# One turn for the sinks of four heads, in a tile shared with the weights' conversion, and new ordering numbers for the first chunks

## Chip, core and metric

The kernel runs on one core of a Trainium2 chip. The core has five engines with queues of their own: TensorE (PE; its loads of the stationary operand are listed as PEld), VectorE (DVE), ScalarE (ACT), GpSimd (POOL) and SyncE (SP), which here only issues DMAs. The metric is the device time of one execution in microseconds, the median of several runs.

## What is computed

Attention with a few sink positions and a sliding window, and behind it a two-layer network whose gate is `h * cos(h)`:

```python
# q, k, v: (4, 8, 768, 64), n_sink = 4, window = 128
scores = q @ k.T / sqrt(D)
keep = (pos_k < n_sink) | ((0 <= pos_q - pos_k) & (pos_q - pos_k < window))
a = softmax(where(keep, scores, -1e9))          # with 1e-9 added to the sum
x = (a @ v).transpose(0, 2, 1, 3).reshape(3072, 512)
h = x @ w_in                                    # w_in (512, 2048)
out = (h * cos(h)) @ w_out                      # w_out (2048, 512)
```

q, k and v are float32. The weights arrive as 64-bit floats, which the kernel turns into pairs of float32 tiles on the chip.

## The kernel before

The 3072 rows are cut into twelve chunks of 256 (`NT`). The chunks that begin a batch of the first three batches come first; the rest follow batch by batch. For a chunk the kernel does attention for eight heads and then the network in eight slots of 256 hidden columns (`NSLOT`).

Products that must be exact to float32 are made of three products of rounded parts (`hi` and `lo`). A slot is 24 hidden products (`h`, line 390), a chain over ACT and DVE (`yt`, `r`, the sine, the gate, `ghi`, `glo`, lines 399 to 429) and 12 output products (`acc`, line 438). `glo` is the last reader of a slot's PSUM bank, so a later slot's hidden products wait for it; the slots of the first two chunks take turns on two banks, the later ones on three.

The weights come in 32 pieces. SP loads a piece into one of two tiles `raw`; DVE builds float32 in one of two tiles `wt` (lines 491, 497, 503), ACT rounds the upper part (line 524), and DVE or POOL subtracts (line 527). Later each piece is loaded once more and checked for very small entries (line 542), which writes its products into a `wt` tile as scratch.

Attention of a head: masked scores (line 856), exponentials (line 865), normalization (line 883 or 885), which is done for groups of four heads in most chunks; PE turns the probabilities (`tp`, line 945), and PE multiplies by v (`av`). The first 24 heads (the three early chunks) go a shorter way: the probabilities stay whole (`pt`), x is split into `xhi` and `xlo`, and PE subtracts the rounded half in PSUM (line 326) before `xlo` is read.

Chunks that are not the first of a batch have sink columns: the eight columns P to SW of the probabilities are taken apart from the window. Before the change a pair of heads shares one turn. `sink_cols` (lines 915, 917) writes the rounded columns of the pair and their remainders to `gc`, a tile of its own of 48 columns per row block; `sink_turn` (line 927) turns the two row blocks on PE into `gp`; `sink_out` copies `gp` to `gt` on ACT or DVE (line 379 or 381); `values` (line 999) then multiplies `gt` by the head's part of `vs`, which `vs_parts` (lines 905, 906) makes once per batch from the first eight rows of v. Rows of `gt` that belong to the other head of the pair meet zeros in `vs`.

Every step is handed to a planner (`Plan.add`) with its possible engines, an assumed duration and a due time; `Plan.order` walks through time and, on each engine, takes the ready step that is due first. The order it finds is written out as it is: the engines' queues are in order on the chip. Due times are sums of numbers in the table `C`; steps that may go to POOL or DVE (such as line 527) are weighed by `POOLPEN`, `POOLF` and others. 160 filler products (`idle`, line 1262) keep PE occupied at the start; they are due last, so the planner puts them wherever PE would have nothing else.

Of the kernel before, what the change touches and what calls it, by code (L numbers as in the profile page):

```python
# [16 lines left out]
P = 128  # L17
NSINK = 8
SW = P + NSINK
GR = 32 + 2 * NSINK  # L20
# [11 lines left out]
    "SAME": -0.209, "SE": -1.813, "SEM": 0.31, "SPE": 0.11, "STEP": 6.272, "T": 6.142, "TE": [-1.145, 6.142, 6.142],  # L32
    "TQ": 6.142, "VE": 5.203, "WARM": 4, "WI": -19.801, "WO": 7.156, "WS": 2.329, "WS2": 0.23, "WT": 2, "XE": 4.169,
    "XV": 2,
# [134 lines left out]
def attn_moe_kernel(ctx, tc, q, k, v, n_sink, window, w_in, w_out, out):  # L169
# [52 lines left out]
    lims = cp.tile([1, 2, 2, 2], F32, name="lims")  # L222
    tiny = cp.tile([P, NC * NSLOT // 2 + NFT], F32, name="tiny")
# [310 lines left out]
    def check_piece(plan, prio, k, src):  # L534

        add, buf = plan.add, plan.buf
        r, bt = buf("raw", C["RAW"]), buf("wt", C["WT"])
        raw, t32 = raws[r.nth], f32(wts[bt.nth])
# [9 lines left out]
        j = add((("DVE", dve(WP) + 0.02),), least, [i, bt], prio, port=True)  # L548
        r.users += [i, j]
        bt.users.append(j)  # L550
        return j
# [59 lines left out]
    def banded_path():  # L611
# [9 lines left out]
        gc = env.gc = ap.tile([P, CB, GR], F32, name="gc")  # L621
        vs = env.vs = ap.tile([P, NP, 2, 2, D], F32R, name="vs")
# [54 lines left out]
        def load_batch_v(o):  # L677
            def fn(e):
                o.vs32 = xb.rearrange("p (n d) -> p n d", d=D)
                for h in range(2):  # L680
                    for dup in range(2):
                        r0 = h * 32 + dup * 8
                        nc.sync.dma_start(
                            out=o.vs32[r0 : r0 + 8], in_=v[o.b, h::2, 0:NSINK, :].rearrange("p s d -> s p d")
                        )
            return fn
# [214 lines left out]
        def vs_parts(o):  # L901
            def fn(e):
                for h in range(2):
                    r = slice(h * 32, h * 32 + 2 * NSINK)
                    nc.vector.tensor_copy(out=vs[r, :, h, 0, :], in_=o.vs32[r])
                    nc.vector.tensor_tensor(
                        out=vs[r, :, h, 1, :], in0=o.vs32[r], in1=f32(vs)[r, :, h, 0, :], op=ALU.subtract
                    )
            return fn

        def sink_cols(o, o1):
            def fn(e):
                j0 = o.sj[0]
                for h, oo in enumerate((o, o1)):
                    nc.vector.tensor_copy(out=gc.bitcast(F32R)[:, j0:, h * 32 : h * 32 + NSINK], in_=oo.p[:, j0:, P:SW])
                for h, oo in enumerate((o, o1)):
                    nc.vector.tensor_tensor(
                        out=gc[:, j0:, h * 32 + NSINK : h * 32 + 2 * NSINK], in0=oo.p[:, j0:, P:SW],
                        in1=gc[:, j0:, h * 32 : h * 32 + NSINK], op=ALU.subtract,
                    )  # L920
            return fn

        def sink_turn(o):
            def fn(e):
                o.gp = ps.tile([GR, NT], F32, name=f"gp_{o.tag}", tag="av")
                for n, j in enumerate(o.sj):
                    nc.tensor.transpose(  # L927
                        out=o.gp[:, n * P : (n + 1) * P], in_=gc[:, j], identity=ident,
                    )
            return fn  # L930

        def sink_out(o, o1):
# [47 lines left out]
        def values(o):  # L980


            def fn(e):
# [10 lines left out]
                if o.sj:  # L994
                    lhs = vs[:, o.pair, o.odd].rearrange("p a d -> p (a d)")
# [39 lines left out]
        w_in_ready, w_out_ready = {}, {}  # L1035
# [4 lines left out]
        def before_softmax(g, o):  # L1040
# [3 lines left out]
            if o.i0 == CB and o.h == 0:  # L1044
# [7 lines left out]
                o.vt = add([("DVE", 1.1)], vs_parts(o), [i, o.bvs], t - T + 3.4, port=True)  # L1052
# [113 lines left out]
        def after_softmax(g, o):  # L1166
# [34 lines left out]
            if o.sj and o.odd == 0:  # L1201
                o1 = heads[g + 1]
                bg, o.bgt, bgp = buf("g", 1), buf("gt", 1), buf("av", 1)
                e1 = add([("DVE", 0.5)], sink_cols(o, o1), o.nm + o1.nm + [bg], t + DA + 0.5, port=True)
                o.bp.users.append(e1)
                o1.bp.users.append(e1)
                e2 = add([("PE", 0.107 * len(o.sj))], sink_turn(o), [e1, bgp], t + DA + 1.0)
                bg.users.append(e2)
                e3 = add([("ACT", act(NT, False)), ("DVE", dve(NT))], sink_out(o, o1), [e2, o.bgt], t + DA + 1.2)
# [10 lines left out]
            if o.sj:  # L1220
                oe = o if o.odd == 0 else heads[g - 1]
# [56 lines left out]
        for m, (t, (ready, ss), piece) in enumerate(sorted(pieces, key=lambda w: w[0])):  # L1278
            i = weight_piece(plan, t, *piece, guard=False, first=m < C["PL"])
            for s in ss:  # L1280
# [185 lines left out]
```

## Time and profile before

| | us |
|---|---|
| runs | 762.22 (median), 759.51 and 763.29 |
| profiled execution | 762.47 |
| its span, first to last instruction | 760.5 |
| PE busy | 737.3 |
| DVE busy | 622.7 |
| ACT busy | 573.9 |
| POOL busy | 104.4 |

The span is about 2 us shorter than the execution's own time, which includes what lies around the program. Busy times are sums over the span: they do not say in which stretch an engine was full, for which the busy time by stretch is read. A row of the timeline has the start, the duration, the engine, the line, the operation and the tiles, and in brackets the idle time before it with what ended it. Durations of PE overlap: a product that lasts 0.28 us can be followed by the next one 0.12 us later, so the distance of two starts says what one costs.

### The profile page before, as it was taken

To read this page: it belongs to the slowest core of one execution; us is meant where nothing else is said; L and a number is where in the kernel's file an instruction comes from. 1 tells how busy PE (TensorE), PEld (TensorE's weight loads), DVE (VectorE), ACT (ScalarE), POOL (GpSimd) and SP (SyncE) were. 2 spreads that over 40 slices of the span, in tenths; PEclk is the share of its full clock that TensorE was granted. 3 is DMA by queue.
4 is the path that set the end of the run, shared out by engine and by line. 5 is a ranking of instruction groups with operands and counts; after the bars stand their busy time and mean duration, and the time that the engine had idled before them with its cause. 6 is when DMAs were issued, how large, how long until landed. Compare 5 with 4: busy or idle time off the path is not lost.

```text
span 760.5 us, 15290 instructions
## 1 busy us (share of the span) xinstructions
PE 737.3 (97%) x5013; PEld 667.1 (88%) x5013; DVE 622.7 (82%) x1645; ACT 573.9 (75%) x1361; POOL 104.4 (14%) x174
## 2 busy tenths in 40 slices
PE   9979998999999999999999999999999999999996
PEld 8767877889989999998999899989999999999995
DVE  6899999678889899999899998987888988864331
ACT  3887986867978878878788788788688788784322
POOL 2101100001121121121221111111021112110000
PEclk9999999999999999999999999999999999999999
DMA  5664563331455446447356443232242233110000
GB/s 155 186 188 153 162 190 117 77 60 32 101 133 130 90 112 173 115 111 195 81 130 168 101 102 55 46 70 35 51 84 48 50 77 55 22 44 2 24 5 33
DMA packets 215673, 71.51 MB, mean 94 GB/s; under 512 B 204320, under 2 KB 204320, under 8 KB 215584
## 3 DMA queue, kind: packets, MB, share of 16 engines
q1 hardware_dynamic: 215296, 70.43, 38.1%
q8 instruction: 42, 0.69, 0.4%
q14 instruction: 47, 0.39, 0.2%
q10 hardware_dynamic: 288, 0.00, 0.0%
HBM read 64.10 MB, written 6.29 MB: 93 GB/s over the span
## 4 chain that ended last, share of the span: by engine, by line
PE 78%; DVE 10%; ACT 5%; DMA 3%; issue 2%; SPq 0%; POOL 0%; DVEq 0%; POOLq 0%; ACTq 0%
PE h L390 30%; PE acc L438 29%; PE av L999 5%; PE s L843 4%; PE tp L945 4%; DVE wt L503 2%; ACT p L865 2%; DVE wt L497 2%; PE idle L1262 1%; DVE p L856 1%; PE gp L927 1%; PE s L787 1%; DMA raw<-in_moe_w_out_dram 1%; DMA raw<-in_moe_w_in_dram 1%; PE av L975 1%
## 5 line engine op out<-in xcount | busy, mean ns | idle before, releaser
L390 PE MATMUL h<-xhi,whi_in 128*128 128x256 f32 x768 | 224.3, 292 | 3.5 <-DVE glo L429 3.5
L390 PE MATMUL h<-xlo,whi_in 128*128 128x256 f32 x768 | 217.3, 283 | 0.0
L390 PE MATMUL h<-xhi,wlo_in 128*128 128x256 f32 x768 | 217.1, 283 | 0.0
L438 PE MATMUL acc<-whi_out,ghi 128*128 128x512 f32 x384 | 159.0, 414 | 0.0
L390 PEld LDWEIGHTS h<-xhi,whi_in 128*128 128x128 f32 x768 | 146.4, 191 | 9.3 <-DVE glo L429 5.1
L438 PE MATMUL acc<-wlo_out,ghi 128*128 128x512 f32 x384 | 151.0, 393 | 0.0
L438 PE MATMUL acc<-whi_out,glo 128*128 128x512 f32 x384 | 150.5, 392 | 0.0
L390 PEld LDWEIGHTS h<-xhi,wlo_in 128*128 128x128 f32 x768 | 146.7, 191 | 3.8 <-issue 0.5
L390 PEld LDWEIGHTS h<-xlo,whi_in 128*128 128x128 f32 x768 | 146.5, 191 | 0.0
L399 ACT ACTIVATE yt<-h 128x512 int32<-128x512 f32 x96 | 57.2, 596 | 67.9 <-PE h L390 67.0
L405 DVE SCALAR_TENSOR_TENSOR r<-h,yt 128x512 f32<-128x512 f32 x96 | 65.8, 685 | 44.1 <-ACT yt L399 44.0
L865 ACT ACTIVATE p<-p,st 128x264 f32<-128x264 f32 (+1 forms) x192 | 93.5, 488 | 0.5
L856 DVE CUSTOM_DVE_ANT_0 p<-s,mk 128x264 f32<-128x264 f32 (+1 forms) x192 | 75.5, 400 | 20.5 <-PE s L843 14.0
L438 PEld LDWEIGHTS acc<-whi_out,glo 128*128 128x128 f32 x384 | 72.1, 188 | 16.2
L438 PEld LDWEIGHTS acc<-whi_out,ghi 128*128 128x128 f32 x384 | 72.6, 189 | 7.7 <-issue 0.7
L438 PEld LDWEIGHTS acc<-wlo_out,ghi 128*128 128x128 f32 x384 | 72.9, 190 | 7.2 <-issue 0.7
L412 ACT ACTIVATE r<-r,neg 128x512 f32<-128x512 f32 x96 | 69.5, 724 | 7.4 <-DVE r L405 6.8
L429 DVE TENSOR_TENSOR glo<-h,ghi 128x512 fp32r<-128x512 f32 x96 | 65.5, 682 | 11.5 <-ACT ghi L423 11.2
L423 ACT CAST ghi<-h 128x512 fp32r<-128x512 f32 x96 | 56.0, 583 | 19.0 <-PE acc L438 18.0
L417 DVE TENSOR_TENSOR h<-h,r 128x512 f32<-128x512 f32 x96 | 66.0, 688 | 3.7 <-ACT r L412 3.4
L843 PE MATMUL s<-r,l 128*128 128x264 f32 (+2 forms) x288 | 60.1, 290 | 1.0 <-DVE st L856 0.7
L898 POOL TENSOR_TENSOR vr<-v,vr 128x192 fp32r<-128x192 f32 (+1 forms) x47 | 29.0, 617 | 215.3 <-ACT vr L893 175.1
(125 smaller groups left out, 1352.8 us busy)
## 6 DMA issues: line engine op xcount, KB each, us to landing
raw<-in_moe_w_in_dram SPq DMA_DIRECT2D x32, 512.0 KB
raw<-in_moe_w_out_dram SPq DMA_DIRECT2D x32, 512.0 KB
xk<-in_k_dram SPq DMA_DIRECT2D x256, 48.0 KB
out_dram<-raw SPq DMA_DIRECT2D x24, 256.0 KB
v<-in_v_dram SPq DMA_DIRECT2D x64, 96.0 KB
xq<-in_q_dram SPq DMA_DIRECT2D x144, 32.0 KB
v<-in_v_dram SPq DMA_DIRECT2D x32, 64.0 KB
xq<-in_q_dram SPq DMA_DIRECT2D x24, 64.0 KB
```

Of the source, the lines that this page charges most:

```text
L390: nc.tensor.matmul(out=o.h[:, t, :], lhsT=w[:, c, fs], rhs=xx[:, c, :], start=(c == 0 and n == 0), stop=(c == NC - 1 and n == 2),)
L399: nc.scalar.activation(out=yt, in_=o.h, func=AF.Copy, scale=INV2PI, bias=0.25)
L405: nc.vector.scalar_tensor_tensor(out=o.r, in0=o.h, scalar=INV2PI, in1=yt, op0=ALU.mult, op1=ALU.subtract)
L412: nc.scalar.activation(out=o.r, in_=o.r, func=AF.Sin, scale=TWOPI_DOWN, bias=quarter)
L417: nc.vector.tensor_tensor(out=o.h, in0=o.h, in1=o.r, op=ALU.mult)
L423: nc.scalar.copy(out=o.ghi, in_=o.h)
L429: e.tensor_tensor(out=o.glo, in0=o.h, in1=f32(o.ghi), op=ALU.subtract)
L438: nc.tensor.matmul(out=x.acc[j], lhsT=gg[:, t, j * P : (j + 1) * P], rhs=w[:, f, :], start=(f == 0 and n == 0), stop=(f == NFT - 1 and n = ...
L843: nc.tensor.matmul(out=o.s_ps[j][:, :w], lhsT=o.l[:, j * P : (j + 1) * P], rhs=r.rearrange("p n s -> p (n s)")[:, c0 : c0 + w], start=(n = ...
L856: nc.vector.tensor_tensor_reduce(out=o.p[:, j, :w], in0=o.s_ps[j][:, :w], in1=masks[min(o.i0 + j, 2)][:, :w], op0=ALU.add, op1=ALU.min, sc ...
L865: nc.scalar.activation(out=o.p[:, j, :w], in_=o.p[:, j, :w], func=AF.Exp, bias=o.lead.st[:, 0, o.nth, j : j + 1], scale=-1.0, accum_out=o. ...
L999: nc.tensor.matmul(out=dst, lhsT=lhs, rhs=rhs, start=(n == 0), stop=(n == len(seq) - 1), skip_group_check=True)
```

## The change

The sink columns of four heads (`GQ`) go into one tile of 64 columns per row block and are turned together. `vs` gets a block per head of a group of four. The rows of `vs` that belong to other heads are no longer simply left at the zero of the first memset: `vs_parts` multiplies whole blocks by a column of `mine`, which is one in the head's own rows and zero in the others. `gc` is no longer a tile of its own but the first tile `wt`, so the first sink columns depend on every weight piece (`wt_done`), and the check of the weights writes its products back over the half of the loaded tile that it has read. The planner's table gets new numbers; two lines of it stand below.

```diff
-GR = 32 + 2 * NSINK
+GQ = 4
+GR = 2 * GQ * NSINK
...
-    "LAG": 4.21, "LB": 49.088, "LEAD": 27.811, "NE": 0.98, "NEH": 24, "NM": 0.98, "NW": 3.409, "NWF": 0.067, "PB": 5,
+    "LAG": 4.21, "LB": 19.541, "LEAD": 28.165, "NE": 0.037, "NEH": 24, "NM": 0.98, "NW": 3.705, "NWF": 0.026, "PB": 5,
-    "PEN": 8.817, "PL": 3, "POOLF": 1.838, "POOLPEN": 0.253, "QE": 5.572, "R": 2, "RAW": 2, "S0": -9.16, "S1": 47.611,
+    "PEN": 8.817, "PL": 3, "POOLF": 1.806, "POOLPEN": -1.93, "QE": 6.213, "R": 2, "RAW": 2, "S0": -8.858,
...
-        nc.gpsimd.memset(env.gc, 0.0)
+        nc.vector.tensor_reduce(
+            out=mine, in_=ident[:GR, :GR].rearrange("p (a h s) -> p h a s", a=2, h=GQ), axis=mybir.AxisListType.XY,
+            op=ALU.max,
+        )
...
             nc.vector.tensor_tensor_reduce(
-                out=t32, in0=top, in1=top, op0=ALU.mult, op1=ALU.max, scale=-1.0, scalar=-3.0e38,
+                out=top, in0=top, in1=top, op0=ALU.mult, op1=ALU.max, scale=-1.0, scalar=-3.0e38,
...
-        gc = env.gc = ap.tile([P, CB, GR], F32, name="gc")
-        vs = env.vs = ap.tile([P, NP, 2, 2, D], F32R, name="vs")
+        gc = f32(wts[0])[:, : CB * GR].rearrange("p (j a r) -> p j a r", j=CB, a=2)
+        vs = env.vs = ap.tile([P, H // GQ, GQ, 2, D], F32R, name="vs")
...
         def vs_parts(o):
             def fn(e):
-                for h in range(2):
-                    r = slice(h * 32, h * 32 + 2 * NSINK)
-                    nc.vector.tensor_copy(out=vs[r, :, h, 0, :], in_=o.vs32[r])
-                    nc.vector.tensor_tensor(
-                        out=vs[r, :, h, 1, :], in0=o.vs32[r], in1=f32(vs)[r, :, h, 0, :], op=ALU.subtract
-                    )
+                part = o.vs32[:GR, : H // GQ]
+                for h in range(GQ):
+                    nc.vector.tensor_scalar(
+                        out=vs[:GR, :, h, 0, :], in0=part, scalar1=mine[:, h : h + 1], scalar2=None, op0=ALU.mult
+                    )
+                for h in range(GQ):
+                    nc.vector.scalar_tensor_tensor(
+                        out=vs[:GR, :, h, 1, :], in0=part, scalar=mine[:, h : h + 1], in1=f32(vs)[:GR, :, h, 0, :],
+                        op0=ALU.mult, op1=ALU.subtract,
+                    )
...
-            if o.sj and o.odd == 0:
-                o1 = heads[g + 1]
+            if o.sj and o.h % GQ == 0:
                 bg, o.bgt, bgp = buf("g", 1), buf("gt", 1), buf("av", 1)
-                e1 = add([("DVE", 0.5)], sink_cols(o, o1), o.nm + o1.nm + [bg], t + DA + 0.5, port=True)
-                o.bp.users.append(e1)
-                o1.bp.users.append(e1)
-                e2 = add([("PE", 0.107 * len(o.sj))], sink_turn(o), [e1, bgp], t + DA + 1.0)
+                cols = []
+                for n in range(0, GQ, 2):
+                    o0, o1 = heads[g + n], heads[g + n + 1]
+                    e1 = add(
+                        [("DVE", 0.5)], sink_cols(o0, o1), o0.nm + o1.nm + (cols or [bg, *wt_done]), t + DA + 0.5 + 0.1 * n, port=True
+                    )
+                    o0.bp.users.append(e1)
+                    o1.bp.users.append(e1)
+                    cols.append(e1)
+                e2 = add([("PE", 0.107 * len(o.sj))], sink_turn(o), [*cols, bgp], t + DA + 1.0)
```

What stands on the engines is the planner's result, so three places show it. The first is PE in the third chunk that has sinks, at heads 0 and 1 of a chunk; `gp` is the turn, `s` the scores of a later head, `h` and `acc` the network, `av` the values. Before:

```order
L945 MATMUL tp_2_1_3915<-ident,p_2_1_3465 128x128 x4
L927 MATMUL gp_2_0_3924<-ident,gc 48x128 x2
L843 MATMUL s_2_5_1_3927<-r_1_2_5_3786,l_2_5_3778 128x264
L843 MATMUL s_2_5_1_3927<-r_1_2_5_3803,l_2_5_3778 128x264
L390 MATMUL h_3884<-xhi_3163,whi_in 128x256
L390 MATMUL h_3884<-xhi_3163,wlo_in 128x256
```

And now:

```order
L935 MATMUL gp_2_0_3922<-ident,wt_72 64x128 x2
L845 MATMUL s_2_5_1_3927<-r_1_2_5_3773,l_2_5_3765 128x264
L845 MATMUL s_2_5_1_3927<-r_1_2_5_3787,l_2_5_3765 128x264
L953 MATMUL tp_2_1_3930<-ident,p_2_1_3453 128x128 x4
L443 MATMUL acc_1_3349<-whi_out,ghi_3759 128x512
L443 MATMUL acc_1_3349<-wlo_out,ghi_3759 128x512
L443 MATMUL acc_1_3349<-whi_out,glo_3768 128x512
L1007 MATMUL av_2_0_3946<-phi_2_0_3867,vr_2_0_3776 128x256
L1007 MATMUL av_2_0_3946<-gt,vs 128x256
```

The turn stands ahead of the second head's own turn instead of behind it and serves four heads; the next `gp` of this chunk, for heads 2 and 3, is gone.

The second place is POOL in the startup, behind its memsets: `wlo` are subtractions of weight pieces (line 527, now 532), `p` normalizations. Before:

```order
L527 TENSOR_TENSOR wlo_in<-wt_72,whi_in 128x512
L527 TENSOR_TENSOR wlo_in<-wt_73,whi_in 128x512 x2
L527 TENSOR_TENSOR wlo_in<-wt_72,whi_in 128x512
L885 TENSOR_SCALAR p_0_2_632<-p_0_2_632,st_0_0_575 128x128
L527 TENSOR_TENSOR wlo_in<-wt_72,whi_in 128x512
L527 TENSOR_TENSOR wlo_out<-wt_72,whi_out 128x512
L527 TENSOR_TENSOR wlo_in<-wt_72,whi_in 128x512
L885 TENSOR_SCALAR p_0_6_816<-p_0_6_816,st_0_4_676 128x128
L527 TENSOR_TENSOR wlo_in<-wt_72,whi_in 128x512
L885 TENSOR_SCALAR p_0_1_1084<-p_0_1_1084,st_0_0_950 128x256
L885 TENSOR_SCALAR p_0_2_1145<-p_0_2_1145,st_0_0_950 128x256
L527 TENSOR_TENSOR wlo_out<-wt_72,whi_out 128x512
```

And now:

```order
L532 TENSOR_TENSOR wlo_in<-wt_72,whi_in 128x512
L887 TENSOR_SCALAR p_0_3_274<-p_0_3_274,st_0_2_272 128x128
L532 TENSOR_TENSOR wlo_in<-wt_73,whi_in 128x512
L532 TENSOR_TENSOR wlo_in<-wt_72,whi_in 128x512
L532 TENSOR_TENSOR wlo_out<-wt_73,whi_out 128x512
L887 TENSOR_SCALAR p_0_4_677<-p_0_4_677,st_0_4_678 128x128
L532 TENSOR_TENSOR wlo_out<-wt_73,whi_out 128x512
L887 TENSOR_SCALAR p_0_7_839<-p_0_7_839,st_0_4_678 128x256
L887 TENSOR_SCALAR p_0_0_946<-p_0_0_946,st_0_0_947 128x128
L887 TENSOR_SCALAR p_0_1_1048<-p_0_1_1048,st_0_0_947 128x256
L887 TENSOR_SCALAR p_0_2_1126<-p_0_2_1126,st_0_0_947 128x256
L836 TENSOR_TENSOR r_0_2_0_1521<-tk_2_0_1474,r_0_2_0_1508 128x408
```

Four of POOL's nine weight subtractions have moved to DVE; normalizations took their places.

The third place is ACT at the end of the first chunk's attention, from the last exponential of the next chunk's first group to the last `xlo`, which the second half of the first slot's hidden products needs. Before:

```order
L865 ACTIVATE p_0_3_635,st_0_0_575<-p_0_3_635,st_0_0_575 128x256
L319 CAST xhi_396<-av_0_6_660 64x256 x2
L524 CAST whi_out<-wt_72 128x512
L883 ACTIVATE p_0_0_574<-p_0_0_574,st_0_0_575 128x128
L379 CAST xlo_432<-av_0_6_660 64x256 x2
```

And now:

```order
L867 ACTIVATE p_0_3_617,st_0_0_521<-p_0_3_617,st_0_0_521 128x256
L529 CAST whi_out<-wt_73 128x512
L529 CAST whi_out<-wt_72 128x512
L324 CAST xhi_400<-av_0_6_687 64x256
L384 CAST xlo_465<-av_0_4_612 64x256
L885 ACTIVATE p_0_0_520<-p_0_0_520,st_0_0_521 128x128
L885 ACTIVATE p_0_1_525<-p_0_1_525,st_0_0_521 128x128
L885 ACTIVATE p_0_2_586<-p_0_2_586,st_0_0_521 128x128
L885 ACTIVATE p_0_2_586<-p_0_2_586,st_0_0_521 128x256
L324 CAST xhi_400<-av_0_6_687 64x256
L384 COPY pt_0_0_729<-tp_0_0_720 128x384
L384 CAST xlo_465<-av_0_6_687 64x256 x2
```

Weight casts, normalizations and a copy now stand among the last two `xhi` and ahead of the last `xlo`.

## Rows read from the trace of the kernel before

**Rows 1.** The page: span, and busy time (share of the span) of each engine.
```profile
span 760.5 us, 15290 instructions
PE 737.3 (97%) x5013; PEld 667.1 (88%) x5013; DVE 622.7 (82%) x1645; ACT 573.9 (75%) x1361; POOL 104.4 (14%) x174
```

**Rows 2.** Busy time by stretch: PE, PEld, DVE, ACT, POOL, granted clock, DMA share, GB/s.
```profile
60.00:80.00 20.00, 18.26 (x124) 16.04 (x123) 19.57 (x37) 16.02 (x34) 4.67 (x3) 1.00 0.48 151
400.00:450.00 50.00, 49.70 (x343) 44.87 (x342) 47.25 (x132) 41.95 (x99) 7.91 (x12) 1.00 0.55 134
450.00:500.00 50.00, 50.00 (x363) 46.51 (x362) 43.62 (x118) 40.32 (x96) 6.33 (x12) 1.00 0.29 55
```

**Rows 3.** PE's waits: total us, times, longest.
```profile
PE h L390 <- DVE glo L429: 3.5, 5, 1.4
PE av L326 <- ACT xhi L319: 2.1, 2, 1.6
```

**Rows 4.** Line 927, the turns: shortest, median, longest ns, first and last start.
```profile
L927 PE MATMUL gp<-ident,gc x64: 269/271/292, 183.2 to 687.3; 128*48 128x128 f32 x64
```

**Rows 5.** Timeline of PE from 302.2 us: start, duration, engine, line, tiles.
```profile
302.29 0.60 PE L945 MATMUL tp<-ident,p 128*128 128x128 f32 x4
302.73 0.38 PE L927 MATMUL gp<-ident,gc 128*48 128x128 f32 x2
302.86 0.49 PE L843 MATMUL s<-r,l 128*128 128x264 f32 x2
```

**Rows 6.** Groups by line and shape: count, busy us, mean ns, idle before.
```profile
L379 ACT CAST gt<-gp 48x256 fp32r<-48x256 f32 x32 | 11.7, 365 | 12.2 <-PE gp L927 12.1
...
L905 DVE CAST vs<-xb 16x256 fp32r<-16x256 f32 x8 | 2.2, 277 | 0.1
L906 DVE TENSOR_TENSOR vs<-xb,vs 16x256 fp32r<-16x256 f32 x8 | 3.3, 414 | 0.3
...
L632 DVE TENSOR_SCALAR mk<-yt,neg 128x128 f32<-128x128 f32 x1 | 0.3, 280 | 0.0
...
L527 DVE TENSOR_TENSOR wlo_in<-wt,whi_in 128x512 fp32r<-128x512 f32 x9 | 6.1, 680 | 0.0
...
L999 PEld LDWEIGHTS av<-plo,vr 128*64 128x64 f32 x208 | 22.7, 135 | 0.0
```

**Rows 7.** Lines 527 and 542: shortest, median, longest ns, first and last start.
```profile
L527 DVE TENSOR_TENSOR wlo_out<-wt,whi_out x14: 673/684/693, 49.6 to 131.4; 128x512 fp32r<-128x512 f32 x14
...
L542 DVE CUSTOM_DVE_ANT_0 wt<-raw x32: 640/683/693, 211.0 to 460.0; 128x512 f32<-128x512 f32 x32
```

**Rows 8.** Timeline of all engines from 120.4 to 123.5 us.
```profile
120.45 0.69 DVE L497 SCALAR_TENSOR_TENSOR wt<-raw,wt 128x512 int32<-128x512 int32 x1
...
120.82 1.46 POOL L527 TENSOR_TENSOR wlo_out<-wt,whi_out 128x512 fp32r<-128x512 f32 x1 [6.75 <-ACT whi_out L524]
...
121.18 1.65 DVE L503 SCALAR_TENSOR_TENSOR wt<-raw,wt 128x512 int32<-128x512 int32 x1
...
122.75 0.68 DVE L429 TENSOR_TENSOR glo<-h,ghi 128x512 fp32r<-128x512 f32 x1
...
123.35 0.41 DVE L856 CUSTOM_DVE_ANT_0 p<-s,mk 128x256 f32<-128x256 f32 x1
123.48 0.39 PE L390 MATMUL h<-xhi,whi_in 128*128 128x256 f32 x1 [1.45 <-DVE glo L429]
```

**Rows 9.** Timeline of all engines from 52.9 us, the end of chunk 0's attention.
```profile
52.94 0.74 ACT L319 CAST xhi<-av 64x256 fp32r<-64x256 f32 x2
...
53.74 0.50 PE L326 MATMUL av<-xhi,gt 128*128 128x512 f32 x1 [1.55 <-ACT xhi L319]
...
54.41 0.73 ACT L379 CAST xlo<-av 64x256 fp32r<-64x256 f32 x2
```

**Rows 10.** Busy time by stretch, columns as in rows 2.
```profile
54.00:57.00 3.00, 2.68 (x12) 2.29 (x12) 2.76 (x8) 2.94 (x8) 0.58 (x1) 0.62 0.94 256
57.00:60.00 3.00, 3.00 (x16) 2.49 (x15) 2.05 (x7) 1.25 (x5) 0.00 (x0) 0.81 0.36 142
```

More of the change, by code (lines that the diff above doesn't have):

```diff
@@ L222, in attn_moe_kernel @@
     lims = cp.tile([1, 2, 2, 2], F32, name="lims")
+    mine = cp.tile([GR, GQ], F32, name="mine")
     tiny = cp.tile([P, NC * NSLOT // 2 + NFT], F32, name="tiny")
@@ L536, in check_piece @@
         add, buf = plan.add, plan.buf
-        r, bt = buf("raw", C["RAW"]), buf("wt", C["WT"])
-        raw, t32 = raws[r.nth], f32(wts[bt.nth])
+        r = buf("raw", C["RAW"])
+        raw = raws[r.nth]
         top = raw[:, :, 1].bitcast(F32)
@@ L547, in check_piece @@
         i = add(dma(1), lambda e: e.dma_start(out=raw.rearrange("p n w -> p (n w)"), in_=src), [r], prio - 6, lat=2.6)
-        j = add((("DVE", dve(WP) + 0.02),), least, [i, bt], prio, port=True)
+        j = add((("DVE", dve(WP) + 0.02),), least, [i], prio, port=True)
         r.users += [i, j]
-        bt.users.append(j)
         return j
@@ L679, in fn @@
                 o.vs32 = xb.rearrange("p (n d) -> p n d", d=D)
-                for h in range(2):
+                for n in range(H // GQ):
                     for dup in range(2):
-                        r0 = h * 32 + dup * 8
-                        nc.sync.dma_start(
-                            out=o.vs32[r0 : r0 + 8], in_=v[o.b, h::2, 0:NSINK, :].rearrange("p s d -> s p d")
-                        )
+                        r = slice(dup * GQ * NSINK, (dup + 1) * GQ * NSINK)
+                        nc.sync.dma_start(out=o.vs32[r, n], in_=v[o.b, n * GQ : (n + 1) * GQ, 0:NSINK, :])
             return fn
@@ L913, in fn @@
                 j0 = o.sj[0]
-                for h, oo in enumerate((o, o1)):
-                    nc.vector.tensor_copy(out=gc.bitcast(F32R)[:, j0:, h * 32 : h * 32 + NSINK], in_=oo.p[:, j0:, P:SW])
-                for h, oo in enumerate((o, o1)):
+                for h, oo in enumerate((o, o1), o.h % GQ):
+                    nc.vector.tensor_copy(
+                        out=gc.bitcast(F32R)[:, j0:, 0, h * NSINK : (h + 1) * NSINK], in_=oo.p[:, j0:, P:SW]
+                    )
+                for h, oo in enumerate((o, o1), o.h % GQ):
                     nc.vector.tensor_tensor(
-                        out=gc[:, j0:, h * 32 + NSINK : h * 32 + 2 * NSINK], in0=oo.p[:, j0:, P:SW],
-                        in1=gc[:, j0:, h * 32 : h * 32 + NSINK], op=ALU.subtract,
+                        out=gc[:, j0:, 1, h * NSINK : (h + 1) * NSINK], in0=oo.p[:, j0:, P:SW],
+                        in1=gc[:, j0:, 0, h * NSINK : (h + 1) * NSINK], op=ALU.subtract,
                     )
@@ L927, in fn, with sink_out @@
                     nc.tensor.transpose(
-                        out=o.gp[:, n * P : (n + 1) * P], in_=gc[:, j], identity=ident,
+                        out=o.gp[:, n * P : (n + 1) * P], in_=gc[:, j].rearrange("p a r -> p (a r)"), identity=ident,
                     )
             return fn
-        def sink_out(o, o1):
+        def sink_out(o):
             def fn(e):
@@ L994, in fn @@
                 if o.sj:
-                    lhs = vs[:, o.pair, o.odd].rearrange("p a d -> p (a d)")
+                    lhs = vs[:, o.h // GQ, o.h % GQ].rearrange("p a d -> p (a d)")
                     seq.append((o.av[:, o.sj[0] * P :], lhs, gt[:, : len(o.sj) * P]))
@@ L1051, in before_softmax @@
                 i = add(dma(4), load_batch_v(o), [o.bv], t - 3 * T, lat=2.3)
-                o.vt = add([("DVE", 1.1)], vs_parts(o), [i, o.bvs], t - T + 3.4, port=True)
+                o.vt = add([("DVE", 1.6)], vs_parts(o), [i, o.bvs], t - T + 3.4, port=True)
                 o.bv.users.append(o.vt)
@@ L1200, in after_softmax @@
             bx.users += [v0, v1]
-            if o.sj and o.odd == 0:
-                o1 = heads[g + 1]
+            if o.sj and o.h % GQ == 0:
                 bg, o.bgt, bgp = buf("g", 1), buf("gt", 1), buf("av", 1)
-                e1 = add([("DVE", 0.5)], sink_cols(o, o1), o.nm + o1.nm + [bg], t + DA + 0.5, port=True)
-                o.bp.users.append(e1)
-                o1.bp.users.append(e1)
-                e2 = add([("PE", 0.107 * len(o.sj))], sink_turn(o), [e1, bgp], t + DA + 1.0)
+                cols = []
[8 more added lines that the diff above has]
+                e2 = add([("PE", 0.107 * len(o.sj))], sink_turn(o), [*cols, bgp], t + DA + 1.0)
                 bg.users.append(e2)
-                e3 = add([("ACT", act(NT, False)), ("DVE", dve(NT))], sink_out(o, o1), [e2, o.bgt], t + DA + 1.2)
+                e3 = add([("ACT", act(NT, False)), ("DVE", dve(NT))], sink_out(o), [e2, o.bgt], t + DA + 1.2)
                 bgp.users.append(e3)
@@ L1220, in after_softmax @@
             if o.sj:
-                oe = o if o.odd == 0 else heads[g - 1]
+                oe = heads[g - o.h % GQ]
                 deps += oe.sinks
@@ L1279, in banded_path @@
             i = weight_piece(plan, t, *piece, guard=False, first=m < C["PL"])
+            wt_done.append(i)
             for s in ss:
```

9 lines of the change are left out of this document (4 added, 5 removed), and 4 rows, old and new, of the table C.

## The prediction

> **What bounds the kernel now.** I read the page first, then the busy time by stretch, then PE's waits, and last the timeline at single places. The page gives PE 97% of a 760.5 us span [rows 1]. By stretch there are two regimes. From about 220 us on PE is busy almost without a gap (50.00 of 50 between 450 and 500), with DVE at 43.6 [rows 2]: there, work taken from PE is time, and work moved between the other engines is not. Before that, DVE is the full engine (19.57 of 20 between 60 and 80 us, where PE has 18.26): it converts the weights, and PE waits on it now and then [rows 2]. PE's list of waits says for what: 3.5 us in five waits of the hidden product for DVE's last read of its PSUM bank, and 2.1 us for ACT's upper half of x [rows 3]. So the change has two parts that can move the end: the transposes that go from PE in the second regime, and the new order in the first.
>
> **Transposes removed.** Before, each pair of heads has two transposes `gp`; after, each four heads have two. There are 64 in the trace [rows 4], so 32 go. One lasts 0.271 us [rows 4], but two in a row span 0.38 [rows 5], so the second began 0.11 after the first; the four of `tp` just before start at 302.29 and give way at 302.73, again 0.11 each. That is 32 x 0.11 = 3.5 us. The lower bound comes from the same place: the score product behind the pair begins at 302.86, 0.13 after the first of them, so a pair takes at least 0.13 and 16 pairs 2.1. I take 3.5, since the row of four agrees and PE is full wherever a `gp` stands but for the first few (183.2 us is the first). The stationary side is 64 columns wide instead of 48; the 64-column loads of `plo` take 0.135 us and cost PE no idle time [rows 6], so I cost that at nothing. The product of sinks with `vs` keeps its 256 columns: nothing.
>
> A page of the Trainium skill would make the gain smaller: TensorE: Matmul & The Clock Gate, section "Back-to-back issue gap", gives about 81 ns for one product of 128 columns in a stream of weight loads and products; by that the 32 would be worth 2.6 us, an estimate from that page. The row says 0.11 each here, and the row decides.
>
> **Copies of the turned sinks.** 16 of 32 ACT copies `gt` go, 0.365 us each [rows 6]: 5.8 us of ACT, which is idle a fifth of that regime [rows 2]. Nothing on the path.
>
> **Sinks of v.** DVE splits them per batch in eight instructions instead of four: before 2 x 0.277 + 2 x 0.414 = 1.38 us, after four products with a per-row factor and four with a subtraction on 128 columns, 0.28 each by the mask row of that shape [rows 6], 2.2 us. That is 0.9 more for each of four batches; three lie where DVE has some 6 us of idle time in 50, one in the startup, where it counts (below). The one reduction `mine` falls into DVE's early wait for a DMA.
>
> **The new waits.** The turn now waits for the columns of all four heads. All four belong to one softmax group before as after, and in PE's order the turn keeps its distance to the first product that needs it (a handful of products, about a microsecond). The first columns also wait for the last weight conversion, since they lie in its tile: the last one starts at 131.4 us [rows 7], the first turn at 183.2 [rows 4], 51 us of cover. Nothing. If that cover were gone, what is queued behind on DVE is the masking of the next heads, and PE would wait for it.
>
> **The check of the weights.** It writes its 32 products back into the loaded tile, every second word, instead of a dense scratch tile. The trace shows no such write; 0.683 us dense [rows 7]. Below, nothing excludes no cost at all; above, I take twice the time, 32 x 0.68 = 21.7 us of DVE between 211 and 460 us. I take no cost, since the conversion that reads every second word of such a tile (0.69 us at 120.45) runs at the pace of the dense subtraction at 122.75 (0.68) [rows 8]. DVE then hides it. The doubled case is a rival below.
>
> **The startup.** Up to the gate product of the eleventh slot the order after gives DVE four more weight subtractions (13 instead of 9, at 0.68 [rows 6]: +2.7), the wider split of v (+0.9) and small copies that ACT gave up (+1.2): +4.8 us by durations. Neighbours start 0.60 apart where one lasts 0.68 (122.75 and 123.35 in [rows 8]), so about +4.2 in time. POOL in turn does 5 weight subtractions instead of 9. Each is dear to DVE: while POOL ran one at 120.82, DVE's shift took 1.65 us instead of 0.69 [rows 8]; over the nine the excess is 5.6 us by the same comparison of rows, 0.62 each. Four fewer return 2.5 us (3.8 if all cost as much as the one shown). So DVE is later by +1.7 (+0.4 to +4.2). ACT has 2.3 us less before the same point. On PE the same 160 fillers stand ahead of the first hidden product, and the work ahead of the thirteenth slot is equal; between, slots change places: the seventh hidden product comes after another slot's output products (4.4 us of PE work), the ninth 4.7 us of work earlier. The order after gives the seventh's bank back later and the ninth's 2 us earlier. The ninth is where PE now waits longest for a bank, 1.45 us [rows 8].
>
> One place looks worse. At the end of chunk 0 ACT now does two weight casts, four normalizations and a copy among the last halves of x, which before went straight through: 0.74 and 0.73 us with 0.7 between them [rows 9]. By the same rows that is some 5.2 us after the last exponential instead of 2.4. PE already waited 1.55 us there [rows 9], and the granted clock then fell: 0.62 over 54 to 57 us, 0.81 over the next three [rows 10], that is half speed, 1.2 GHz, for about 3.4 us, 1.7 us lost. Against that the masks that start these exponentials stand 0.7 us earlier on DVE, and one blocking POOL operation less stands before them.
>
> DVE's +1.7 and ACT's -2.3 pull apart; I put the startup at 0. Its bounds: -3.5 if all five waits for a bank go [rows 3], +4.2 if DVE's whole lag reaches PE.
>
> **Sum.** The profiled execution took 762.47 us, its span 760.5. 762.47 - 3.5 + 0 = 759.0. The median of the three runs shown is 762.22, 0.25 below the profiled one, so 758.7 against it. A measurement of this kernel tells about 0.5% from no change, 3.8 us: below 758.4 is faster, above 766.0 slower. The forecast lies within, close to the edge.
>
> **Rivals.**
> (a) The startup gains too. For it: the ninth slot's bank comes earlier and POOL blocks DVE less. Against: DVE has more to do. Price -2 to -5, so 753.5 to 757, with 755.2 if the five waits go.
> (b) The startup gives the gain back: DVE's lag reaches PE whole, for it is the full engine there. +1.5 to +4.2: 760.2 to 763.
> (c) Slower: the write into every second word halves DVE in the check, between 211 and 460 us. DVE is at 47.25 of 50 at its fullest there [rows 2], so some 14 us are idle in 250; 21.7 - 14 = 8 us reach PE, 758.7 + 8 = 767. It decides from about 1.1 us an instruction instead of 0.68. Against: the reads of that stride cost nothing.
> (d) The change does not do what it says: the turns were never on the path, and 762.2 stands. The full stretches of PE speak against it.
> A second kind of slower lies in the tail of (b): the longer wait at the end of chunk 0 lets the clock fall twice.
>
> **Chances.** Forecast, startup within 1.5 us of zero: 0.45, of which 0.16 below 758.4. (a) 0.27. (b) and (d) 0.20. (c) and the tail of (b) 0.08. So faster 0.43, within 0.5% 0.49, slower 0.08. The range from 754.5 to 763.3 holds the forecast, nearly all of (b) and (d) and most of (a), and leaves out (c) and some 0.08 of (a).
>
> **What would show it.** Transposes: 32 rows of `gp`, 0.27 us each, and PE's sum lower by 3.5 us against the same fillers. Startup: PE's busy time in the stretches up to 140 us; a sum of its waits there within 1.5 us of the one before is the forecast. DVE: nine conversions on POOL become five, and rows of 1.65 us become rarer. Check: its rows at 0.68 us. If PE has idle time above 1 us behind 220 us, the argument on the second regime is wrong.

## The result and the profile after

The changed kernel takes 753.63 us (median of five runs, 752.05 to 756.41) against 762.22; the ratio is 0.990, with a 95% interval from 0.987 to 0.993. A second measurement of the same file gave 754.32 against 761.72, ratio 0.991 (0.989 to 0.993). So it is 7.4 to 8.6 us faster, where 3.5 were forecast. 753.63 lies 0.9 us below the lower end of the range and the second median 0.2 below it: the sign was right, the forecast is the wrong one of the cases, and rival (a) with its 753.5 to 757 is what happened. The interval of the ratio, put on 762.22, runs from 752.3 to 756.9 us: the range is missed by less than the noise, the forecast of 758.7 is not. One execution of a kernel below, `vs3`, took 2549.78 us and is left out of its median.

The profiled execution of after took 756.41 us, the slowest of the five; its span is 754.6. The page, as in [rows 1]:

```profile
span 754.6 us, 15212 instructions
PE 734.6 (97%) x4981; PEld 665.4 (88%) x4981; DVE 619.2 (82%) x1658; ACT 565.0 (75%) x1338; POOL 108.0 (14%) x184
```

Busy time by stretch, columns as in [rows 2]; the last two lines are new:

```profile
60.00:80.00 20.00, 18.71 (x124) 16.37 (x123) 19.59 (x44) 19.19 (x45) 1.27 (x1) 1.00 0.56 169
...
400.00:450.00 50.00, 49.34 (x341) 44.96 (x340) 45.27 (x130) 40.88 (x98) 9.62 (x16) 1.00 0.47 113
450.00:500.00 50.00, 50.00 (x363) 46.52 (x361) 42.93 (x117) 41.84 (x101) 9.14 (x16) 1.00 0.30 59
...
48.00:60.00 12.00, 8.94 (x48) 7.43 (x47) 10.41 (x29) 8.19 (x25) 0.00 (x0) 0.86 0.50 154
84.00:90.00 6.00, 5.78 (x28) 4.57 (x29) 5.33 (x15) 4.64 (x13) 0.00 (x0) 0.72 0.50 173
```

The two regimes are as before. New is the 0.72 over 84 to 90 us: a second stretch at half speed (1.2 GHz), 3.4 us long (6 us x 0.28 / 0.5), beside the one near 52 us; PE had waited 0.75 and 1.60 us ahead of it.

PE's waits up to 150 us, total us, times, longest. First after:

```profile
PE h L395 <- DVE pt L386: 2.8, 1, 2.8
PE h L395 <- DVE glo L434: 2.6, 2, 1.6
PE s L789 <- DVE st L858: 1.6, 2, 1.2
PE qk L765 <- DMA xq<-in_q_dram: 1.5, 1, 1.5
```

and of before the rows that answer or have gone:

```profile
PE h L390 <- DVE glo L429: 3.2, 4, 1.4
PE av L326 <- ACT xhi L319: 2.1, 2, 1.6
PE s L787 <- DVE kz L381: 1.8, 1, 1.8
...
PE av L975 <- DMA v<-in_v_dram: 0.8, 1, 0.8
```

The waits for banks hardly changed (3.2 to 2.6). What went is ACT's upper half of x (2.1), DVE's copy of k (1.8) and a load of v (0.8); what came is one wait of 2.8 us for the copy of the turned probabilities, at the first hidden product.

The single steps, rows by line (shortest, median, longest ns, first and last start), of after:

```profile
L935 PE MATMUL gp<-ident,wt x32: 270/272/273, 184.6 to 675.0; 128*64 128x128 f32 x32
...
L547 DVE CUSTOM_DVE_ANT_0 raw<-raw x32: 642/686/1496, 203.7 to 442.4; 128x512 f32<-128x512 f32 x32
...
L502 DVE SCALAR_TENSOR_TENSOR wt<-raw,wt x32: 681/693/848, 10.4 to 128.4; 128x512 int32<-128x512 int32 x32
```

32 turns at 0.272 us, as forecast. The check that writes every second word has a median of 0.686, against 0.683 dense in [rows 7]; rival (c) falls with that row. The second step of a conversion (line 502) now takes 0.85 us at worst; before, as line 497, up to 1.76. Before has five rows of DVE between 1.65 and 1.76 us up to 140 us, after none; its longest are 1.37 and 1.05.

### The profile page after: what moved, and what is told of

It reads as the page before. It is cut to its first block, busy times and chain, and to the rows that moved or that the text cites. A ratio compares the mean times of both kernels' runs of the same rounds, so it can differ in the third digit from the quotient of the medians.

```text
span 754.6 us, 15212 instructions
## 1 busy us (share of the span) xinstructions
PE 734.6 (97%) x4981; PEld 665.4 (88%) x4981; DVE 619.2 (82%) x1658; ACT 565.0 (75%) x1338; POOL 108.0 (14%) x184
## 4 chain that ended last, share of the span: by engine, by line
PE 78%; DVE 14%; DMA 3%; issue 2%; ACT 2%; SPq 1%; POOL 0%; DVEq 0%; POOLq 0%; ACTq 0%
PE h L395 31%; PE acc L443 30%; PE av L1007 5%; PE s L845 4%; PE tp L953 4%; DVE wt L502 2%; DVE p L858 2%; DVE wt L508 2%; PE idle L1275 1%; PE av L983 1%; PE s L789 1%; DVE wt L496 1%; DMA v<-in_v_dram 1%; DVE glo L434 1%; DVE p L887 1%
## 5 line engine op out<-in xcount | busy, mean ns | idle before, releaser
L395 PEld LDWEIGHTS h<-xhi,whi_in 128*128 128x128 f32 x768 | 146.3, 190 | 12.9 <-DVE glo L434 6.1
L443 PE MATMUL acc<-whi_out,ghi 128*128 128x512 f32 x384 | 157.1, 409 | 0.0
L443 PEld LDWEIGHTS acc<-whi_out,glo 128*128 128x128 f32 x384 | 72.1, 188 | 16.5
L900 POOL TENSOR_TENSOR vr<-v,vr 128x192 fp32r<-128x192 f32 (+1 forms) x50 | 32.4, 649 | 223.2 <-ACT vr L895 173.4
```

Source lines behind the costliest of these rows:

```text
L395: nc.tensor.matmul(out=o.h[:, t, :], lhsT=w[:, c, fs], rhs=xx[:, c, :], start=(c == 0 and n == 0), stop=(c == NC - 1 and n == 2),)
L443: nc.tensor.matmul(out=x.acc[j], lhsT=gg[:, t, j * P : (j + 1) * P], rhs=w[:, f, :], start=(f == 0 and n == 0), stop=(f == NFT - 1 and n = ...
```

## The experiments

Twelve runs were made. One mark serves for most of them: the first hidden product of the thirteenth slot (PE's products `h`, counted by 24). In before, after and all kernels below whose order agrees with one of them up to the first turn, PE has the same work ahead of that mark, but for fillers where told, so its time measures the startup, and the stretch from it to PE's last product the rest. Idle time is counted from PE's first instruction. Each mark is that of one profiled execution: `again` and `turns5`, whose startups are the same, have 145.13 and 144.83.

| kernel | median, us | before in the same job | mark | PE idle ahead of it | mark to PE's end, less idle |
|---|---|---|---|---|---|
| before | 762.22 | | 148.97 | 13.0 | 602.7 |
| after, its two measurements | 753.63, 754.32 | 762.22, 761.72 | 146.40, 145.13 | 10.6, 11.6 | 600.1, 600.1 |
| struct | 762.94 | 761.72 | | 13.7 | |
| table | 765.98 | 761.72 | | 16.5 | |
| struct11 | 758.74 | 762.21 | 148.35 | 11.9 | 600.9 |
| table16 | 757.16 | 762.21 | 147.06 | 9.5 | 603.2 |
| after11 | 763.70 | 762.21 | | 15.5 | |
| after27 | 758.83 | 761.96 | | 16.2 | |
| turns5 | 766.94 | 761.72 | 144.83 | 10.5 | 613.0 |
| fill24 | 755.55 | 762.21 | 144.69 | 8.6 | 600.1 |
| vs3 | 769.55 | 761.96 | 149.35 | 13.2 | 602.3 |
| pool0 | 754.36 | 761.96 | 144.34 | 10.6 | 600.0 |
| late | 754.09 | 762.23 | 144.52 | 9.7 | 599.8 |

### The two halves of the change alone

`again` is after unaltered. `struct` is after with the table `C` of before; `table` is before with the table of after.

> The changed kernel once more, unaltered, for a second profile and a time on the same chip as the other three. Theory A (the profile of after is typical but for its second clock fall at 85 us): 752 to 755 us, PE's idle time up to 150 us some 10 to 11 us, and one clock fall fewer in a run of the median. Theory B (part of the 8.6 us is chance between executions): 755 to 758 us.

> The structure of after (turns of four heads, sink columns in the weights' tile, check in place, wider split of v) with the offsets of before. Theory A (the turns are worth 32 x 0.08 = 2.6 us by PE's sum of pitches, the offsets the rest, and the two add): 759.5 us, between 758 and 761. The prediction (turns 0.11 each, offsets nothing): 758.7 at the place of 753.6, so the whole gain of after is here: 754 to 755. Theory C (new offsets are only needed because the structure disturbs the old order): 762 or slower.

> The kernel before with the offsets of after and nothing else. Theory A (offsets and turns add): 756 to 757.5 us, with PE's idle time up to 150 us near the 10.5 us of after instead of 13.0. The prediction (offsets nothing): 762. Theory C (the offsets fit only the structure that they were chosen for): 762 or slower, with the idle time of before or more.

The second look bears the first out: 754.32 us and one fall of the clock instead of two, with 11.6 us of idle time ahead of the mark, somewhat over the 10 to 11 expected. But neither half gains. The structure alone is 1.2 us above before, ratio 1.001 (0.9998 to 1.0023), the offsets alone 4.3 us, 1.005 (1.003 to 1.007); together they are 7.4 faster. Theory A and the prediction both failed here, and theory C has the signs. The traces show what went with it. In `struct` the granted clock falls four times in the startup where before has one fall; these are the stretches, columns as in [rows 2]:

```profile
54.00:60.00 6.00, 5.50 (x27) 4.28 (x26) 5.46 (x14) 3.93 (x11) 1.27 (x1) 0.72 0.60 178
88.00:94.00 6.00, 5.71 (x19) 4.14 (x19) 5.97 (x15) 5.14 (x13) 2.11 (x3) 0.72 0.29 88
112.00:118.00 6.00, 5.56 (x29) 5.39 (x30) 4.64 (x11) 5.54 (x14) 1.54 (x4) 0.72 0.90 221
122.00:128.00 6.00, 5.91 (x25) 4.64 (x26) 5.90 (x15) 3.69 (x10) 1.06 (x1) 0.72 0.28 89
```

The falls alone don't explain the loss: of the eleven executions of `struct` the one with the highest mean granted clock, 0.999, took 763.57 us, about as long as the profiled one (763.98 at 0.991).

In `table` DVE takes six steps of weight conversions ahead of the one subtraction that frees a bank, one of them held up by POOL, and PE waits 5.57 us. Timeline from 81 us (start, duration, engine, line, tiles):

```profile
81.06 0.42 DVE L491 TENSOR_SCALAR wt<-raw 128x512 int32<-128x512 int32 x1
81.52 0.69 DVE L497 SCALAR_TENSOR_TENSOR wt<-raw,wt 128x512 int32<-128x512 int32 x1
82.24 0.69 DVE L503 SCALAR_TENSOR_TENSOR wt<-raw,wt 128x512 int32<-128x512 int32 x1
...
83.67 1.26 POOL L527 TENSOR_TENSOR wlo_out<-wt,whi_out 128x512 fp32r<-128x512 f32 x1 [12.93 <-ACT whi_out L524]
83.76 1.72 DVE L497 SCALAR_TENSOR_TENSOR wt<-raw,wt 128x512 int32<-128x512 int32 x1
85.51 0.69 DVE L503 SCALAR_TENSOR_TENSOR wt<-raw,wt 128x512 int32<-128x512 int32 x1
86.12 0.68 DVE L429 TENSOR_TENSOR glo<-h,ghi 128x512 fp32r<-128x512 f32 x1
...
86.95 0.55 PE L390 MATMUL h<-xhi,whi_in 128*128 128x256 f32 x1 [5.57 <-DVE glo L429]
```

### One planned number

The orders of `struct` and before part within PE's first 40 rows, far ahead of anything that the turns touch. Of all that the structure alters in the plan, only one number stands that early: the split of v is planned at 1.6 us instead of 1.1. So three kernels alter that number alone; the split itself stays as it is.

```diff
-  o.vt = add([("DVE", 1.6)], vs_parts(o), ...)   # struct -> struct11, after -> after11
+  o.vt = add([("DVE", 1.1)], vs_parts(o), ...)
-  o.vt = add([("DVE", 1.1)], vs_parts(o), ...)   # table -> table16
+  o.vt = add([("DVE", 1.6)], vs_parts(o), ...)
```

With it PE's order in `struct11` is that of before, and in `table16` that of after, row by row up to the first turn; in `after11` it is that of `table`.

> Like struct (structure of after, offsets of before), but the planner is told 1.1 us for the split of v, as in before, and not 1.6. The split itself is unaltered. The order of PE is then that of before up to the first turn at 183 us. Theory D (struct lost its 3 us because that one planned duration gives the startup another order, with four falls of the clock instead of one; with the order held, what is left is the turns): 758.5 us, between 757.5 and 759.5, one clock fall before 150 us. Rival E (the real work of the structure disturbs the startup: wider split of v, the reduction): 761 to 763, with PE's idle time up to 150 us above the 13.0 of before.

> Like table (before with the offsets of after), but the planner is told 1.6 us for the split of v. The order of PE is then that of after up to the first turn. Theory D: the startup of after with the 64 turns of before, so after plus 32 x 0.1 us: 757.5 us, between 756.5 and 758.5, with no wait of 5.6 us at the third slot. Rival E: 762 or slower, as table.

> After, with one number altered: the planner is told 1.1 us for the split of v instead of 1.6. Theory D: the startup falls into the order that table had, so table less 32 turns: 762.8 us, between 761.5 and 764, with a wait of over 5 us for a bank at the third slot. Rival E (an estimate of half a microsecond of one instruction in some thousand can't matter): 754 to 755.

All three came within 1 us of theory D: 758.74 for 758.5, 757.16 for 757.5, 763.70 for 762.8. With the order held, the parts add: the structure gives 3.5 us (ratio 0.995, 0.993 to 0.997), the new order 5.0 (0.993, 0.991 to 0.995), 8.5 together, and after has 7.4 to 8.6. And the same kernel with one planned duration altered by half a microsecond loses 9.4 us, from 754.3 to 763.7. PE's waits up to 150 us go with the order, not with the structure; of `struct11` and then of `table16`:

```profile
PE h L395 <- DVE glo L434: 3.2, 4, 1.5
PE av L331 <- ACT xhi L324: 2.1, 2, 1.6
PE s L789 <- DVE kz L386: 1.8, 1, 1.8
```

```profile
PE h L390 <- DVE glo L429: 2.6, 2, 1.6
PE h L390 <- DVE pt L381: 2.4, 1, 2.4
```

The trace of after shows the split at 2.87 us in the startup (from its first start at 43.15 to the next instruction's at 46.02) and 1.83 later, so neither planned number is true. The last kernel of this group tells the planner 2.7:

```diff
-  o.vt = add([("DVE", 1.6)], vs_parts(o), ...)   # after -> after27
+  o.vt = add([("DVE", 2.7)], vs_parts(o), ...)
```

> After, with the planner told 2.7 us for the split of v, which is what the trace of after shows for it (2.9 with one row held up by POOL), instead of 1.6. Theory H (the startup is as good as the plan's numbers are true): 752 to 754. Theory I (any number that is altered deals the order of the startup anew, and the offsets were chosen for one order): anywhere between 755 and 764, and likely slower than after by over 1 us.

758.83 us, 4.5 above `again`, with 16.2 us of PE idle ahead of the mark: theory I. A truer number is no better; it deals another order than the one that the offsets and 1.6 give together.

### The price of a turn

```diff
-  for n, j in enumerate(o.sj):               # after -> turns5
+  for n, j in list(enumerate(o.sj)) * 5:
```

> After, with every turn of the sinks issued five times in a row to the same bank (160 transposes instead of 32), in the same order of everything else. It measures the price of one on a full PE. The prediction's 0.11 us: +14.1 us over after. PE's sum of pitches in the two traces, 0.08 us: +10.2. Theory C (the turn is hidden beside other work): less than 3.

12.6 us over `again` for 128 more turns: 0.099 each, between the two values expected; by the last column of the table 12.9 / 128 = 0.10. The timeline of PE (columns as in [rows 5]) shows it in place:

```profile
300.54 1.25 PE L935 MATMUL gp<-ident,wt 128*64 128x128 f32 x10
301.55 0.49 PE L845 MATMUL s<-r,l 128*128 128x264 f32 x2
```

Ten turns hold the next product up by 1.01 us.

### The pace of the startup

Does a microsecond of DVE reach PE there? `vs3` issues the split of v three times over, in all four batches; `late` takes the first batch's split out of the startup; `pool0` gives DVE the five subtractions that POOL has.

```diff
+  for _ in range(3):                          # after -> vs3: around the eight instructions of vs_parts
...
-  e.tensor_tensor(out=lo, in0=t32, in1=f32(hi), op=ALU.subtract)          # after -> pool0
+  nc.vector.tensor_tensor(out=lo, in0=t32, in1=f32(hi), op=ALU.subtract)
...
+  if o.b == 0:                                # after -> late, in vs_parts
+      env.late = todo                         # its eight instructions, held back
+      return
...
+  for _ in range(2 if o.m >= 9 and env.late else 0):    # in g_lo, behind the subtraction
+      f, h = env.late.pop(0)
+      f(h)
```

> After, with the eight instructions that split v's sinks issued three times in a row (each batch; the first lies at 43 us, ahead of the wait of the scores at 47 us, the other three behind 290 us); nothing else moves. By the rows of after the sixteen added ones cost DVE 4.3 us at 46 us. Theory F (DVE sets the pace of the startup, as the prediction's bound for DVE's lag has it): all of it reaches the end, 758.3 us, between 757 and 759.5. Theory G (DVE is full but PE's waits there are set by single places, so that most of a delay is taken up by later slack): 754 to 756.

> After, with the five subtractions of the weights that run on POOL issued on DVE at the same place of the program; all else stands. DVE gets 5 x 0.60 = 3.0 us more. The prediction's step (each of them on POOL holds DVE up by some 0.6 us, so moving it is even): 754 us, between 753 and 755, with fewer rows of DVE above 1 us before 90 us. Rival (POOL takes them off DVE at no price): 757, if DVE's time reaches PE.

> After, with the first batch's split of v taken from DVE's place at 43 us and put, two instructions at a time, behind the lower halves of the gate of the slots ten to thirteen (143 to 165 us), where PE is full and DVE has some 5 us idle in 20; its first reader comes at 185 us. All other instructions keep their order. In again the eight rows take 2.93 us of DVE at 43 us. Theory F (DVE's time in the startup reaches the end whole, as 4.2 us of it did in vs3): 751.1 us, between 750 and 752.5, and the thirteenth slot's first hidden product 2 to 3 us earlier than 145.1. Theory J (the slope holds only for delays: with less work on DVE, ACT's chain or a load is late next): 753 to 754.5.

`vs3` met theory F at the mark and missed the total. The split at 43 us became 3.75 us longer (6.61 instead of 2.86 in `again`), and the mark came 4.22 us later: all of it reaches PE. 3.87 of that stand at the first hidden product already. The fall of the clock beside it is longer too, 10.2 us instead of 3.4, and no run takes its share apart. But the median is 15.2 above `again`. Each of the three later batches, which were to cost nothing, made PE wait for the sinks' columns, 2.7, 2.3 and 2.9 us where `again` has no such wait, and one more stretch at half speed followed, at 601 us. Timeline at the first of them:

```profile
303.89 0.86 DVE L912 SCALAR_TENSOR_TENSOR vs<-xb,mine,vs 64x128 fp32r<-64x128 f32 x3
...
305.25 0.26 DVE L926 TENSOR_TENSOR wt<-p,wt 128x16 f32<-128x16 f32 x2
...
305.66 0.38 PE L936 MATMUL gp<-ident,wt 128*64 128x128 f32 x2 [2.73 <-DVE wt L926]
```

The two repeats add 3.67 us there, so the cover is 0.7 to 1.4 us, not the 6 idle ones of the stretch.

`pool0` is even: 754.36 against 754.32. The conversions lose their long rows, as the first step (line 496) shows, of after and then of `pool0`:

```profile
L496 DVE TENSOR_SCALAR wt<-raw x32: 398/420/1051, 10.0 to 128.0; 128x512 int32<-128x512 int32 x32
```

```profile
L496 DVE TENSOR_SCALAR wt<-raw x32: 396/420/428, 9.2 to 125.9; 128x512 int32<-128x512 int32 x32
```

The five subtractions cost DVE 3.4 us (0.68 each). The rows of the conversions give back 1.8 of that, and the split of v, which had one long row in after, 1.0 (1.84 us instead of 2.86). So what DVE gains it spends on the five subtractions; here a subtraction on POOL freed next to nothing on DVE. The Trainium skill, Perfetto Trace Analysis, section "Optimizing Scalar/DVE Operations", says of these two engines that they share a read port, so that moving work from one to the other might not help; this run agrees, with 754.36 against 754.32 us for five subtractions.

`late` is no faster, 754.09: theory J. The first hidden product does come 1.7 us earlier (49.69 instead of 51.39), and with it all up to the fifth slot (82.20 instead of 83.97). Of the 2.86 us the rest is taken up by the next thing due, a load of v that wasn't in time:

```profile
PE h L395 <- DVE pt L386: 1.4, 1, 1.4
...
PE av L996 <- DMA v<-in_v_dram: 1.1, 1, 1.1
```

Then 1.6 us are lost again between the fifth slot and the sixth: this profile has its stretch at half speed at 83 us and none at 52. At the mark 0.6 are left. Why the other executions gain no more isn't shown; the profiled one, at 753.56, is the fastest of the five. So a delay of 3.75 us on DVE there reached the mark whole, and of 2.86 us taken away 0.6 did.

### The clock

`fill24` puts 24 products of the filler's kind on PE, into the filler's own bank, ahead of the first hidden product:

```diff
+  for _ in range(24 if (o.m, t, half) == (0, 0, 0) and env.fillw is not None else 0):
+      nc.tensor.matmul(out=env.idle, lhsT=env.fillw, rhs=..., start=True, stop=True)
```

> After, with 24 products of the filler's kind (0.11 us each, 2.6 us in all) put on PE ahead of the first hidden product, where PE waits 2.8 us; every other instruction stands where it stood. If PE's idle stretch is what lets the granted clock fall at 52 us (3.4 us at half speed, 1.7 us lost), the fall goes or shrinks: 752.6 us, between 751.5 and 753.5. If the fall has another cause, 754.3 as after; if the fillers run into the next product, up to 755.

The clock stays up in this profile, but the time doesn't follow: 755.55 us, ratio 0.991 (0.989 to 0.993), no different from after. The stretch of after stands above with 0.86; that of `fill24` is

```profile
48.00:60.00 12.00, 11.51 (x80) 10.06 (x79) 11.66 (x32) 9.48 (x29) 0.00 (x0) 1.00 0.55 159
```

That the idle stretch caused the fall is not shown by this. In `pool0` PE waits 2.60 us at the same place (50.51 us), and that profile has no fall there. The mean granted clock runs from 0.993 to 0.999 over the five executions of after and from 0.994 to 0.999 over the six of `fill24`, so executions of one kernel differ in it by as much as the two kernels do.

What the fall is worth there can be read. From the first slot's first product to the second's PE takes 8.13 us in `again` and 8.12 in `turns5`, which have the fall, and 7.25 in `fill24` and 7.24 in `pool0`, which don't: 0.9 us, where 3.4 us at half speed could cost 1.7. In place of the rest PE waits 0.48 us for ACT's upper half of x in both. In `fill24` the fillers also hold the first product up by 0.41 us, so the mark is 0.44 us earlier than in `again` and 0.14 than in `turns5`. Its total says little about the fall: behind the mark this profile has a wait of 1.5 us for DVE, at 420 us, that `again` doesn't have.

The fall at 84 us is another matter: from the fifth slot's first product to the sixth's PE takes 6.71 us in the profile of after and 5.05 in that of `again`, which has no fall there. These are the first products, of after and then of `again`:

```profile
84.22 0.39 PE L395 MATMUL h<-xhi,whi_in 128*128 128x256 f32 x1 [1.60 <-DVE glo L434]
...
90.93 0.47 PE L395 MATMUL h<-xhi,whi_in 128*128 128x256 f32 x1
```

```profile
83.97 0.39 PE L395 MATMUL h<-xhi,whi_in 128*128 128x256 f32 x1 [1.60 <-DVE glo L434]
...
89.02 0.47 PE L395 MATMUL h<-xhi,whi_in 128*128 128x256 f32 x1
```

That is 1.66 us, the whole price of 3.4 us at half speed. The other profiles agree: 6.66 in `late` and 6.69 in `pool0` with the fall, 5.05 to 5.06 in `turns5`, `fill24` and `vs3` without, and 7.94 in `table16`, where it lasts 6.8 us. It comes in some executions of one and the same order of PE and not in others, even of one file (after and `again`). The same two waits, 0.7 to 0.8 and 1.6 us, stand ahead of that place in all of them, so these waits don't decide it alone.

## Why the prediction was right and wrong

**What bounds the kernel**: right in both regimes. Behind 220 us PE's longest wait in after is 0.74 us, below the bound of 1 us that was set.

**Transposes, 3.5 with a lower bound of 2.1**: right within its bounds, a little high. With one order, 32 turns fewer shorten the stretch behind the mark by 1.8 us (before to `struct11`) and 3.1 (`table16` to after); one turn more costs 0.10. The 3.5 of the medians of `struct11` has more in it than turns: its mark is 0.6 earlier, and in the profile of before the span outlasts PE's last product by 6.8 us, in all others by 5.8 to 6.0. The figure of 2.6 us from the Trainium skill, TensorE: Matmul & The Clock Gate, section "Back-to-back issue gap", lies between 1.8 and 3.1: setting it aside for a pitch of 0.11 was not borne out.

**Startup, 0 with bounds of -3.5 and +4.2**: the step that failed. By the medians `table16` measures the new order alone at -5.0, outside the bound. At the mark itself the gain is smaller: `again` is 3.8 us earlier than before, `turns5` 4.1, and 0.6 of that came with the structure (`struct11`). `table16` is 1.9 earlier in its profile, which is its slowest execution, with 2.9 us lost to the long fall at 83 us. So the startup itself lies close to the bound, and a part of the 5.0 behind it or in the spread. The working compared the sums of DVE's and ACT's work up to a place, +1.7 and -2.3, and let them cancel. DVE did have more to do (its durations up to 135 us add up to 139.2 us in after and 135.8 before; since they overlap, that is 121.8 and 119.9 us of busy time, 1.9 more where 1.7 was forecast), and the last weight conversion ends at the same time (131.7 and 132.1). But PE waits for single rows and not for sums, and the new order puts those rows ahead: 13.0 us of idle time ahead of the mark become 10.6 in after, with one fall of the clock more, and 11.6 in `again`, with none more. The bound of -3.5 counted the five waits for banks alone; the waits that went were others, which stood in the same list. Hidden in PE's busy time there was more: where a run of output products begins, the second follows the first by 0.23 to 0.42 us, but at three places of before (73.07, 117.49 and 131.59 us) by 0.63; after has none of 0.63. One of the three:

```profile
117.49 0.80 PE L438 MATMUL acc<-whi_out,ghi 128*128 128x512 f32 x1
118.12 0.39 PE L438 MATMUL acc<-wlo_out,ghi 128*128 128x512 f32 x1
```

`struct11` has the three as well and `table16` none, so they go with the order; what makes them isn't shown.

**Rival (a)** had the size, with half of the reason: the wait for the ninth slot's bank did fall, from 1.45 to 0.10 us, but the waits for banks together gave 0.6, and the rest came from waits that the rival doesn't name. **The end of chunk 0**, which looked worse, is worse in its first wait (2.8 us against 1.55) and made up for by the next slot (59.7 against 60.2 us). The second clock fall, put into the tail of (b), came in the profiled execution, near 85 us and not there.

**Split of v, 0.9 in the startup and nothing later**: too large. With the order held the split takes 0.3 to 0.4 us more (1.84 in `struct11` against 1.51 in before, 2.86 in `again` against 2.49 in `table16`, from its first start to the next instruction's), and the mark of `struct11` is not later than that of before. The reason for "nothing later", "some 6 us of idle time in 50", is refuted by `vs3`. **POOL's subtractions, 0.6 us of DVE each**: borne out by `pool0`, where moving them was even at 0.68 each. **Check in place, 0**: borne out by its rows.

What stays open is which of the changed offsets give the new order its gain. They act on one list, and a change to any one deals the startup anew, as one planned duration did, so no run took them apart. Nor did a run remove the wait for the weights' tile, which shows no idle time in after.

## What to carry to other kernels

Where a planner orders the work, a change of structure and a change of its numbers can't be judged one at a time: here neither alone gained, and both together gained 8 us; to price the structure, hold the order (one planned duration did it), and then choose the numbers anew. Where several engines are nearly full, don't let sums of work cancel: list every wait of the full engine, also those that are not long, and ask of each whether the new order moves the row that ends it. Price a step by repeating it in place: it shows cover that an average of idle time only promises (0.7 to 1.4 us under a step, where the stretch had 6).

## What the hardware showed beside that

- 3.4 us at half speed cost 0.9 us where PE otherwise waits for ACT (8.1 us against 7.25 for one slot) and 1.6 to 1.7 where it doesn't (6.66 to 6.71 against 5.05). Of two executions of one file one had a fall near 85 us and one had none, behind the same waits.
- On DVE, 128x512 products written back over every second word take 0.686 us, 0.683 dense.
- Five subtractions of 1.3 us on POOL, moved to DVE at 0.68 each, left the time as it was (754.32 and 754.36 us).
